# Norm sums of batches 2 and 3 moved beside the first `w_gate` jobs, and their result passed through a row in DRAM

## The chip, the cores and the metric

One Trainium2 chip, one of its cores. The metric is the device time of one execution in microseconds. The engines are called PE (TensorE, with its weight loads as PEld), DVE (VectorE), ACT (ScalarE), POOL (GpSimd) and SP (SyncE, which here only issues transfers).

## The reference

```python
# attention: batch 4, 12 heads, 448 tokens, head size 64
scores = scale * np.matmul(q, k.transpose(0, 1, 3, 2)) - np.log(S)
attn = 1.0 / (1.0 + np.exp(-scores))
x = np.matmul(attn, v)                # tokens x 768 after the heads are joined
# first gated layer, 768 -> 1536 -> 768
rms = np.sqrt(np.mean(x * x, axis=-1, keepdims=True) + 1e-06)
xn = x / rms * rms_g
g = xn @ w_gate
silu = g * (1.0 / (1.0 + np.exp(-g)))
x = silu * (xn @ w_val) @ w_out
# second layer, 768 -> 2048 -> 768
h = x @ w_in
out = (h - np.tanh(h)) @ w_out2
```

All of it in float32. The change concerns `rms`: one number for each of the 4 x 448 tokens.

## The kernel before

The tokens lie along the free dimension: a `unit` tile is 128 features by 448 tokens of one batch, so x of a batch is six units. The attention runs batch by batch, six pairs of heads each: line 612 makes scores, line 619 their sigmoid, line 642 the product with v. Each pair gives one unit of x. `x_end` squares it on ACT and adds it on DVE to a unit `sq`; for batches 2 and 3 it also spills x to DRAM (line 669).

Then the layers run in two halves, batches 0 and 1 and then 2 and 3 (`BATCHES`). A float32 product is three matmuls on a high and a low part of each operand. The work is a list of jobs: `seven_units` (line 978) makes two output chunks of `w_gate`, `w_val` or `w_in` for two batches with seven block products in place of eight, `set_units` (line 921) does the same for a set of `w_out` or `w_out2`, `plain_units` (line 1003) a set without that saving. The right factors of x for a half take 42 units (`xs`: 3 chunk pairs x 7 products x high and low part), those of a set 28 (`moe`: 2 x 7 x 2).

The norm of one batch is three functions. `norm(b)` multiplies the four 112-token pieces of `sq` with a column of ones (line 677, four float32 matmuls, which the trace shows as eight records), which leaves the sums as 112 x 4 numbers in a PSUM bank; DVE scales them (line 681), and POOL raises them to the power -0.5 into `rc` (line 683). `clear_norm(b)` writes the whole bank once (line 331). `spread_norm(b)` has to bring these numbers into a row along the free dimension on all 128 partitions: DVE makes diagonal pieces from the identity (line 698, four per batch), PE multiplies them with ones (line 702), and ACT copies the bank to a unit `rstd` (line 706). `x_whole` (line 770) then scales x by `rms_g` and `rstd` on DVE.

The order in which everything is issued is written out by a planner, the class `Plan`. Each operation is given to it with its engine, an assumed duration, what it reads and writes, and how long after its end its result is there (`after`; `LAND` and `FAR` for transfers). It keeps a clock per engine, starts what can start soonest, and among those within 150 ns the one with the earliest due time. Due times go back from PE's operations in program order, so PE keeps nearly that order. `plan.later` gives an operation a later due time. Operations up to `WINDOW` = 500 places behind the oldest open one may start, those that open a buffer of a kind in `CLOSELY` (`xr`, `sq`, `acc`, `accs`, `again`) only up to 120. Buffers come from shared pools: 72 units (`N_UNIT`) for all kinds of unit, each kind with a limit of its own (`sq` 3, `rstd` 2, `xs` 42), and eight PSUM banks. Every engine then runs its list in order and waits on semaphores.

What surrounds the change: `mixed` puts side work between the units of the attention, and the main loop puts the lists of `beside` between the units of the jobs from `j0` up to `j1`:

```python
    mixed(attn_units(3), [lambda: norm(2), lambda: clear_norm(2)], [u for j in range(AHEAD) for u in (*by_dve(conv(j)), lambda j=j: load(j + AHEAD))], rows_b[at[2]:])
    norm(3)
    clear_norm(3)
    gates.clear()
    ...
        (last["Av", BATCHES[0]], first["Ag", BATCHES[1]], [lambda: [spread_norm(b) for b in BATCHES[1]], *x_units("A", BATCHES[1], True)], BEHIND),
```

So the sums of batch 2 stand in the attention of batch 3, those of batch 3 right behind it, and both are spread much later, beside the last `w_val` job of the first half, ahead of the reloads of x (`reload_x`, line 713) and its scaling for the second half.

Of the kernel before, what the change touches and what calls it, by code (L numbers as in the profile page):

```python
# [8 lines left out]
F32 = mybir.dt.float32  # L9
# [12 lines left out]
P = 128  # L22
# [237 lines left out]
def tile_sigmoid_attention_moe_moe(  # L260
# [38 lines left out]
    def bank(kind="mm"):  # L299
        return slot(kind, ps_p, [P, 512], F32, "ps")  # L300
# [82 lines left out]
    def load(j):  # L383
        if j >= len(jobs) or jobs[j][1] != BATCHES[0] or jobs[j][3] or is_early(jobs[j][0], jobs[j][2]):
            return
        ph, _, i, _ = jobs[j]
        raws[j] = [load_raw(PAIRS[ph][0][2 * i + e]) for e in range(2)]
# [84 lines left out]
    def conv(j):  # L472
        if j >= len(jobs):
            return []
        ph, bs, i, blocks = jobs[j]
        if blocks in (SET, PLAIN):
            return set_factors(j)
        if (ph, i) in stored:
            return again_units(j)
        return pair_units(ph, i, raws.pop(j), j)  # L480
# [190 lines left out]
    def norm(b):  # L671
        sq = sqs.pop(b)
        ps = bank("nm")
        ms, rc = (Slot(None, lambda t=t: norm_p.tile([TK, 4], F32, tag=t, name=t)) for t in ("ms", "rc"))
        def sums(e):
            for i in range(4):
                nc.tensor.matmul(  # L677
                    ps.tile[:TK, i:i + 1], lhsT=sq.tile[:, i * TK:(i + 1) * TK], rhs=ones[:, 0:1], start=True, stop=True)

        add({"PE": (1500, False)}, sums, [sq["t"]], [ps["t"]], stream="norm")  # L680
        add(dve(4), lambda e: nc.vector.tensor_scalar(
            out=ms.tile, in0=ps.tile[:TK, :4], scalar1=1.0 / DM, scalar2=EPS, op0=ALU.mult, op1=ALU.add), [ps["t"]], [ms["t"]])
        add({"POOL": (950, True)}, lambda e: nc.gpsimd.tensor_tensor(out=rc.tile, in0=ms.tile, in1=expo, op=ALU.pow),
            [ms["t"]], [rc["t"]])
        rcs[b] = rc, ps

    def clear_norm(b):
        ps = rcs[b][1]
        add({"PE": (250, False)}, lambda e: whole_bank(ps.tile), [], [ps["t"]], stream="norm")

    def spread_norm(b):
        (rc, _), ps2 = rcs.pop(b), bank("nm")
        dg = unit("sq")
        r = rstd[b] = unit("rstd")

        def spread(e):
            for i in range(4):
                nc.vector.tensor_scalar(
                    out=dg.tile[:TK, i * TK:(i + 1) * TK], in0=id_sb, scalar1=rc.tile[:, i:i + 1], scalar2=None, op0=ALU.mult)

        def rows(e):
            nc.tensor.matmul(ps2.tile[:, :S], lhsT=ones[:TK, :], rhs=dg.tile[:TK, :], start=True, stop=True)  # L702

        add({"DVE": (760, True)}, spread, [rc["t"]], [dg["t"]])
        add({"PE": (1500, False)}, rows, [dg["t"]], [ps2["t"]], stream="norm")
        add(act(S, psum=True), lambda e: nc.scalar.copy(r.tile, ps2.tile[:, :S]), [ps2["t"]], [r["t"]])
# [344 lines left out]
    def attn_units(b):  # L1051
        units = []
        for at in range(b * HP, (b + 1) * HP, 2):
            for x in (at, at + 1):
                units.append(lambda x=x: pair_qk(*pairs[x], (0, 1)))
                units.append(lambda x=x: (get_ready(x + 3), pair_qk(*pairs[x], (2, 3))))
            for x in (at, at + 1):
                units.append(lambda x=x: (pair_av(*pairs[x]), pair_end(*pairs[x])))
        return units
# [29 lines left out]
    def by_dve(units):  # L1089
        def run(u):  # L1090
            plan.copies_by = "DVE"
            u()
            plan.copies_by = None

        return [lambda u=u: run(u) for u in units]

    def mixed(units, *others):


        at = [0] * len(others)  # L1100
        for u in units[:2]:
            u()
        units = units[2:]
        for n, u in enumerate(units):
            u()
            for k, o in enumerate(others):
                while at[k] < (n + 1) * len(o) // len(units):
                    plan.later = BESIDE
                    o[at[k]]()
                    plan.later = 0  # L1110
                    at[k] += 1
# [5 lines left out]
    mixed(attn_units(2), [lambda: norm(1), lambda: clear_norm(1), lambda: spread_norm(1), *x_units("A", BATCHES[0], False)], rows_b[at[1]:at[2]])  # L1117
    for j in range(AHEAD):
        load(j)
    mixed(attn_units(3), [lambda: norm(2), lambda: clear_norm(2)], [u for j in range(AHEAD) for u in (*by_dve(conv(j)), lambda j=j: load(j + AHEAD))], rows_b[at[2]:])  # L1120
    norm(3)
    clear_norm(3)
    gates.clear()


# [1 line left out]
    first = {(ph, bs): [j for j in range(len(jobs)) if jobs[j][0] == ph and jobs[j][1] == bs][0] for ph in ("Ag", "C") for bs in BATCHES}  # L1127
    last = {(ph, bs): [j for j in range(len(jobs)) if jobs[j][0] == ph and jobs[j][1] == bs][-1] for ph in ("Av", "C") for bs in BATCHES}
    beside = [
        (last["Av", BATCHES[0]], first["Ag", BATCHES[1]], [lambda: [spread_norm(b) for b in BATCHES[1]], *x_units("A", BATCHES[1], True)], BEHIND),  # L1130
        (last["Av", BATCHES[1]], first["C", BATCHES[0]], x_units("C", BATCHES[0], True), BEHIND),
        (last["C", BATCHES[0]], first["C", BATCHES[1]], x_units("C", BATCHES[1], True), BEHIND),
# [97 lines left out]
```

## Time and profile before

| | us |
|---|---|
| median of 3 runs | 1059.64 (1057.77 to 1060.39) |
| profiled execution | 1060.05 |
| its span, first to last instruction | 1058.2 |
| PE busy | 1045.9 |
| attention, up to about | 165 |
| first half of `w_gate`, `w_val` and `w_out` | about 165 to 400 |

The span is that of one profiled execution. Busy time counts a stretch once, also where matmuls overlap. In the chain of waits each piece starts where the one before it released it, so a piece of PE is the time that PE's stream really moved on. In the timeline a row is a run of like instructions, and the brackets hold how long the engine stood before it and what ended that. In the table of stretches the columns are the stretch and its length, the busy us of PE, PEld, DVE, ACT and POOL with their instructions, the granted clock (1.00 is full), the DMA engines' busy share and GB/s. `L324` and `L331` are helpers (copies, and the writing of a whole bank), `SPq` is SP's queue.

### The profile page before, as it was taken

How to read it: one execution, taken by the hardware profiler on the slowest of the kernel's cores; microseconds unless marked ns; L12 is line 12 of the kernel's file. 1: busy time of each engine (PE TensorE's matmuls, PEld its weight loads, DVE VectorE, ACT ScalarE, POOL GpSimd, SP SyncE). 2: the span in 40 equal slices, each digit the busy share in tenths (PEclk: the TensorE clock that was granted, in tenths of full speed). 3: DMA queues.
4: the chain of work that ended last, by engine and by line, in shares of the span. 5: the costliest groups of instructions: out<-in, count | busy, mean ns of one | idle time of the engine just before them, and what ended most of it. 6: DMA issues, size and time to landing. Idle time of an engine off the chain costs nothing.

```text
span 1058.2 us, 15120 instructions
## 1 busy us (share of the span) xinstructions
PE 1045.9 (99%) x5148; PEld 876.2 (83%) x5148; DVE 766.9 (72%) x1212; ACT 689.4 (65%) x1247; POOL 139.7 (13%) x194
## 2 busy tenths in 40 slices
PE   9999999999999999999999999999999999999998
PEld 3434447999999889999999989999988899999997
DVE  1328976975976895875885777888886888667756
ACT  5766765666675755665665656677675777666652
POOL 1211100000004022111113021000303120003030
PEclk9999999999999999999999999999999999999999
DMA  6888787766759979697879589557959891849393
GB/s 195 275 282 273 239 287 259 280 209 225 255 208 204 343 185 294 205 297 264 290 248 313 166 223 275 209 205 282 199 215 273 241 263 60 281 123 201 113 198 130
DMA packets 105869, 245.64 MB, mean 232 GB/s; under 512 B 27072, under 2 KB 59328, under 8 KB 105792
## 3 DMA queue, kind: packets, MB, share of 16 engines
q1 hardware_dynamic: 82224, 179.63, 50.2%
q0 software_dynamic: 23264, 64.89, 25.0%
q8 instruction: 40, 0.66, 0.3%
q14 instruction: 37, 0.30, 0.1%
q10 hardware_dynamic: 304, 0.16, 0.1%
HBM read 151.44 MB, written 93.19 MB: 231 GB/s over the span
## 4 chain that ended last, share of the span: by engine, by line
PE 88%; issue 5%; DMA 4%; DVE 1%; ACT 1%; POOL 1%; SPq 0%; POOLq 0%; DVEq 0%; ACTq 0%
PE ps L978 43%; PE ps L921 24%; PE ps L612 7%; PE ps L642 7%; PE ps L1003 5%; DMA out<-unit 2%; DMA cv<-wB 1%; DMA wt<-in_w_in 1%; PE ps L331 1%; DVE unit L857 1%; POOL out L795 0%; DVE unit L726 0%; PE ps L702 0%; PE ps L677 0%; ACT wt L324 0%
## 5 line engine op out<-in xcount | busy, mean ns | idle before, releaser
L978 PE MATMUL ps<-unit,wt 128*128 128x448 f32 x2520 | 522.1, 366 | 5.0 <-DVE unit L857 3.6
L978 PEld LDWEIGHTS ps<-unit,wt 128*128 128x128 f32 x2520 | 472.2, 188 | 48.5 <-DVE unit L857 4.7
L921 PE MATMUL ps<-unit,wt 128*128 128x448 f32 x1512 | 313.8, 366 | 0.0
L921 PEld LDWEIGHTS ps<-unit,wt 128*128 128x128 f32 x1512 | 283.8, 188 | 24.3 <-ACT ps L324 0.3
L407 DVE TENSOR_TENSOR wt<-cv,wt 128x768 fp32r<-128x768 f32 (+1 forms) x244 | 215.8, 892 | 76.1 <-ACT wt L324 70.9
L324 ACT CAST wt<-cv 128x768 fp32r<-128x768 f32 (+1 forms) x236 | 185.3, 787 | 108.3 <-PE ps L978 64.0
L324 ACT COPY unit<-ps 128x448 f32<-128x448 f32 x300 | 156.4, 534 | 130.0 <-PE ps L978 49.8
L726 DVE TENSOR_TENSOR unit<-unit 128x448 fp32r<-128x448 f32 x252 | 153.0, 620 | 28.9 <-ACT unit L324 13.4
L324 ACT CAST unit<-unit 128x448 fp32r<-128x448 f32 x252 | 137.9, 567 | 30.8 <-DVE unit L731 9.1
L857 DVE TENSOR_TENSOR unit<-ps,unit 128x448 f32<-128x448 f32 x168 | 103.5, 621 | 47.6 <-PE ps L978 27.6
L731 DVE TENSOR_TENSOR unit<-unit 128x448 f32<-128x448 f32 x144 | 87.4, 619 | 20.1 <-DMA unit<-sumB 10.2
L619 ACT ACTIVATE unit<-ps 128x448 f32<-128x448 f32 (+1 forms) x192 | 84.8, 582 | 6.2 <-PE ps L612 5.9
L612 PE MATMUL ps<-wt 64*128 64x448 f32 (+1 forms) x384 | 77.4, 546 | 0.0
L642 PE MATMUL ps<-unit,cv 128*64 128x448 f32 (+1 forms) x384 | 75.1, 542 | 0.0
L795 POOL DMA_DIRECT2D sumB<-unit x48 | 41.4, 945 | 255.0 <-DVE unit L857 157.2
L396 DVE SCALAR_TENSOR_TENSOR cv<-wt,zero 128x768 uint32<-128x768 uint32 x68 | 64.8, 953 | 11.6 <-ACT zero L324 6.6
L612 PEld LDWEIGHTS ps<-wt 64*128 64x128 f32 (+1 forms) x384 | 32.9, 173 | 39.6 <-issue 29.2
L642 PEld LDWEIGHTS ps<-unit,cv 128*64 128x64 f32 (+1 forms) x384 | 26.3, 136 | 47.5 <-issue 38.0
L1003 PE MATMUL ps<-unit,wt 128*128 128x448 f32 x288 | 60.3, 366 | 1.4 <-ACT unit L324 0.8
L324 ACT CAST zero<-wt 128x768 f16<-128x768 bf16 x52 | 56.1, 1078 | 8.6 <-DVE cv L396 4.6
L1003 PEld LDWEIGHTS ps<-unit,wt 128*128 128x128 f32 x288 | 53.8, 188 | 7.0 <-ACT unit L324 1.6
L665 DVE TENSOR_TENSOR unit<-unit 128x448 f32<-128x448 f32 x20 | 12.5, 623 | 62.3 <-ACT unit L658 62.3
(44 smaller groups left out, 427.1 us busy)
## 6 DMA issues: line engine op xcount, KB each, us to landing
wt<-in_w_out POOLq DMA_DIRECT2D x28, 768.0 KB, 7.4
cv<-wD SPq DMA_DIRECT2D x56, 384.0 KB, 4.9
cv<-wB SPq DMA_DIRECT2D x36, 384.0 KB, 5.4
wt<-in_w_in SPq DMA_DIRECT2D x16, 768.0 KB, 6.8
sumB<-unit POOLq DMA_DIRECT2D x48, 224.0 KB, 6.9
wD<-cv POOLq DMA_DIRECT2D x28, 384.0 KB, 5.6
wt<-in_w_gate SPq DMA_DIRECT2D x12, 768.0 KB, 5.1
wt<-in_w_val SPq DMA_DIRECT2D x12, 768.0 KB, 4.9
```

Source lines behind the costliest of these rows:

```text
L324: add(engines, lambda e: (nc.scalar.copy if e == "ACT" else nc.vector.tensor_copy)(to(), of()), reads, writes)
L396: add(dve(NW, psum=False), lambda e: nc.vector.scalar_tensor_tensor(out=c.tile.bitcast(U32), in0=r.tile[:, :NW, 1], scalar=13, in1=z.tile, ...
L407: add({**dve(n, psum=False), **pool(n)}, lambda e: ENG[e].tensor_sub(lo(), of(), hi().bitcast(F32)), [*reads, *kh], [*kl])
L612: nc.tensor.matmul(ps[i, c].tile[:n, :S], lhsT=t.tile[rows, at:at + n], rhs=t.tile[rows, :S], start=True, stop=True)
L619: add(act(S, psum=True), lambda e: nc.scalar.activation(to.tile[at:at + n, :S], ps.tile[:n, :S], AF.Sigmoid, bias=-math.log(S), scale=1.0 ...
L642: nc.tensor.matmul(ps.tile[i * D:(i + 1) * D, :S], lhsT=v.tile[:n, c, i, :], rhs=a[c][i].tile[:n, :], start=(c == 0), stop=(c == 3))
L726: add({**pool(S), **dve(S, psum=False)}, lambda e: ENG[e].tensor_sub(t["l"].tile, of.tile, t["h"].tile.bitcast(F32)), [of["t"], kh], [kl])
L731: add({**dve(S, psum=False), **pool(S)}, lambda e: ENG[e].tensor_sub(t.tile, x.tile, y.tile), [x["t"], y["t"]], [t["t"]])
L857: add(dve(S), lambda e: nc.vector.tensor_add(t.tile, ps.tile[:, :S], t.tile), [ps["t"], t["t"]], [t["t"]])
L921: nc.tensor.matmul(ps.tile[:, :S], lhsT=part(a), rhs=x[b].tile, start=n in (1, 5) and kp == 0 and q == 0, stop=kp == n_kp - 1 and q == 2, ...
L978: nc.tensor.matmul(ps.tile[:, :S], lhsT=part(a), rhs=x[b].tile, start=n in ((1, 2, 5) if opening else (1, 5)) and i == 0 and q == 0, stop= ...
L1003: nc.tensor.matmul(ps.tile[:, :S], lhsT=wt, rhs=a[p].tile, start=start and i == 0, stop=stop and i == 2, skip_group_check=True)
```

## The change

`norm` and `clear_norm` of batches 2 and 3 leave the attention and become four pieces of side work, spread evenly over the first two jobs (a `w_gate` and a `w_val` job). For these batches `norm` also writes `rc` to a row in DRAM with a transfer on SP, element by element, and `spread_norm` is one transfer on SP that loads this row to all 128 partitions of `rstd`. The diagonal pieces, the product with ones and the copy remain for batches 0 and 1 only. Places and due times of the later list in `beside` are as they were.

```diff
@@ norm(b), after the power
-        rcs[b] = rc, ps
+        if b in BATCHES[0]:
+            rcs[b] = rc, ps
+            return
+        d = Slot(None, lambda: dram_p.tile([1, S], F32, name=f"rstd{b}"))
+        rcs[b] = d, ps
+        add({"SP": (650, False)}, lambda e: nc.sync.dma_start(
+            out=d.tile.rearrange("o (i p) -> (o p) i", p=TK), in_=rc.tile), [rc["t"]], [d["t"]], after=15000)
@@ spread_norm(b), at its start
+        if b in BATCHES[1]:
+            d, _ = rcs.pop(b)
+            r = rstd[b] = unit("rstd")
+            add({"SP": (650, False)}, lambda e: nc.sync.dma_start(out=r.tile, in_=d.tile[0].partition_broadcast(P)), [d["t"]], [r["t"]], after=FAR)
+            return
@@ attention of batch 3
-    mixed(attn_units(3), [lambda: norm(2), lambda: clear_norm(2)], [u for j in range(AHEAD) for u in (*by_dve(conv(j)), lambda j=j: load(j + AHEAD))], rows_b[at[2]:])
-    norm(3)
-    clear_norm(3)
+    mixed(attn_units(3), [u for j in range(AHEAD) for u in (*by_dve(conv(j)), lambda j=j: load(j + AHEAD))], rows_b[at[2]:])
@@ beside
+        (first["Ag", BATCHES[0]], first["Ag", BATCHES[0]] + 2, [lambda b=b, f=f: f(b) for b in BATCHES[1] for f in (norm, clear_norm)], BEHIND),
```

## Rows read from the trace of the kernel before

**Rows 1.** The page, busy time of each engine, and TensorE's granted clock in 40 slices.

```profile
PE 1045.9 (99%) x5148; PEld 876.2 (83%) x5148; DVE 766.9 (72%) x1212; ACT 689.4 (65%) x1247; POOL 139.7 (13%) x194
...
PEclk9999999999999999999999999999999999999999
```

**Rows 2.** Who waited for whom, TensorE, whole span: us, times, longest us.

```profile
PE ps L978 <- DVE unit L857: 3.6, 3, 2.2
PE ps L331 <- POOL mark L1061: 1.9, 1, 1.9
```

**Rows 3.** The chain that ended last, attention of batch 3: start us, us, what.

```profile
124.71 5.46 PE ps L612 x28
130.17 0.88 PE ps L677 x8
131.05 0.93 PE ps L612 x4
...
138.14 3.96 PE ps L612 x20
142.10 0.29 PE ps L331
142.40 2.46 PE ps L612 x12
```

**Rows 4.** The same chain, where the attention ends and `w_gate` begins.

```profile
167.63 0.69 PE ps L677 x8
168.32 0.72 PE ps L978 x3
...
169.25 58.02 PE ps L978 x285
```

**Rows 5.** The same chain, end of the first `w_gate`/`w_val` half, batches 0 and 1.

```profile
319.88 8.05 PE ps L921 x40
...
329.47 14.55 DMA cv<-wB
...
359.14 0.76 PE ps L702 x2
359.90 0.61 PE ps L978 x3
...
361.26 3.87 PE ps L978 x19
```

**Rows 6.** Timeline, DVE, three places: start us, us, instruction [idle before, releaser].

```profile
168.36 0.16 DVE L681 TENSOR_SCALAR ms<-ps 112x4 f32<-112x4 f32 x1 [1.49 <-PE ps L677]
...
328.12 1.61 DVE L698 TENSOR_SCALAR unit<-id_sb,rc 112x112 f32<-112x112 f32 x8
...
361.59 1.27 DVE L770 SCALAR_TENSOR_TENSOR unit<-unit,g_sb 128x448 f32<-128x448 f32 x2
```

**Rows 7.** Groups by line, whole span: count, busy us, mean ns, idle before.

```profile
L683 POOL TENSOR_TENSOR rc<-ms,expo 112x4 f32<-112x4 f32 x4 | 4.7, 1167 | 36.9 <-DVE ms L681 36.9
...
L706 ACT COPY unit<-ps 128x448 f32<-128x448 f32 x4 | 2.1, 525 | 1.6 <-PE ps L702 1.6
```

**Rows 8.** Three stretches: engines' busy us (instructions), granted clock, DMA share, GB/s.

```profile
165.00:230.00 65.00, 65.00 (x324) 59.73 (x325) 51.79 (x83) 40.89 (x66) 1.01 (x1) 1.00 0.66 233
290.00:318.00 28.00, 28.00 (x140) 25.89 (x139) 21.17 (x33) 19.74 (x34) 0.00 (x0) 1.00 0.59 208
325.00:350.00 25.00, 22.84 (x113) 20.71 (x112) 15.02 (x30) 12.82 (x22) 7.22 (x10) 1.00 1.08 290
```

**Rows 9.** SP's transfers of lines 1073 and 713: duration, landing, min/median/max.

```profile
L1073 SPq DMA_DIRECT2D g_sb<-in_rms_g x1: 1831/1831/1831, 17.4 to 17.4; - x1
...
L713 SPq DMA_DIRECT2D unit<-x x12: 319/382/1247, 331.0 to 381.4; - x12
...
DMA to landing us min/median/max: 3.0/4.3/17.4
```

**Rows 10.** Timeline, SP, the first weight loads for set 0.

```profile
188.65 1.75 SPq L521 DMA_DIRECT2D cv<-wB  x2
```

## The prediction

> **What bounds the kernel now.** I read the page first, then the list of who waited for whom, then the chain of waits around the three places that the diff touches, then the rows of the moved and removed instructions. The page [rows 1] shows TensorE (PE) busy for 1045.9 of 1058.2 us, at the upper of its two clock levels (2.4 GHz) in every slice; VectorE (DVE) has 72%, ScalarE (ACT) 65%. Only 12.3 us are free of matmuls. Its longest named waits [rows 2] are 1.9 us at the start and one of 2.2 later. In the chain [rows 4] the `w_gate`/`w_val` products run 285 matmuls in 58.02 us, 203.6 ns each, without a wait. So TensorE in program order sets the time, and an instruction taken out of its stream is worth what it holds there, unless a wait behind it grows. One such wait stands near the change: the chain leaves TensorE there for a weight load, `cv<-wB`, issued at 329.47 us and 14.55 us on its way [rows 5], and behind it TensorE stands for the 2.2 us. The profiled execution took 1060.05 us, 1.85 more than its span; the three timed runs have their median 0.41 lower, at 1059.64. I sum against 1060.05 and take off 0.41 at the end.
>
> **What is removed: two diagonal products (batches 2 and 3).** In the chain [rows 5] the first starts at 359.14 and the matmuls behind the second at 361.26: 2.12 us, of which the three matmuls between them take 3 x 0.2036 = 0.61. So the two products hold TensorE for 1.51 us. They are the program's last use of line 702 in a stretch where the chain stays on TensorE, so I take all of it: -1.51. The ends are 0, if the time comes back as a wait, and -1.51. Off the path, DVE loses its 8 diagonal pieces, 1.61 us in all [rows 6], and ACT two copies of 525 ns [rows 7]. I count both at nothing: the chain at that time runs through the weight load, not through DVE.
>
> **What is moved: norm sums and clearing of batches 2 and 3.** Batch 3 is moved by little. In the trace it already stands between `w_gate` products [rows 4]: 167.63 to 169.25 is 1.62 us, less three matmuls (0.61) is 1.01 us for sums and clearing with what they cost at their edges. It keeps this price a few products later: 0. Batch 2 does leave the attention [rows 3]. There its sums take 0.88 us and split a run of score matmuls into 28 and 4, which take 5.46 + 0.93 = 6.39; by the runs of 28 and 12 (5.46 and 2.46, so 0.1875 each) an unsplit run of 32 takes 6.21, so the split costs 0.18. The clearing takes 0.29 and splits 20 from 12: 3.96 + 2.46 - 6.21 = 0.21 more. Together 1.56 us in the attention against 1.01 beside `w_gate`: -0.55. Ends: 0, if the new place costs the same, and -1.56, if it costs nothing. At the new place the sums wait for nothing, since both sums of squares are done before the first of these jobs.
>
> The in-order engines get new waits there. DVE's 160 ns scaling stood 1.49 us for the sums of batch 3 [rows 6]; batch 2 now adds one like it. Behind it stand conversions of weights and the closing of PSUM banks; DVE is busy 51.79 of 65 us in that stretch [rows 8], so 13 us of free time cover 1.5. Without that cover it would be 1.5 us of TensorE per batch. GpSimd's power (1.17 us [rows 7]) finds its engine idle: it is all that ran there in those 65 us [rows 8]. A norm bank stays taken from the sums to the clearing, some ten products or 6.5 us for each batch, beside the three banks of each of two overlapping jobs: seven of eight, so 0; if it comes up short, a product waits for one ACT copy, 0.53 us [rows 7].
>
> **What is added on SP's queue.** Per batch, one store of 448 numbers as single 4-byte pieces, and one load that spreads the row over 128 partitions. The trace has no such store. Its nearest rows [rows 9] are the reloads of x (0.32 to 1.25 us on SP, 3.0 to 17.4 us to landing) and the load of `g_sb`, 128 runs of 24 bytes: 1.83 us on SP. By the number of pieces the latter gives an estimate of 1.83 x 448/128 = 6.4 us, so a store holds SP for 0.3 to 6.4 us, plus a wait for GpSimd of a microsecond or two; I take 1.8, the `g_sb` row. Behind it are weight loads; the nearest to their use are the `cv<-wB` loads from 188.65 us [rows 10], wanted by the first set product, at 169.25 + 58.02 = 227.27 [rows 4]. That is 34 us of cover against at most 13 for both stores: 0. Without that cover SP's time would come straight onto TensorE.
>
> The spread load has the shape of the reloads of x, and I take their time. Its place matters more. The planner may start an operation up to 500 work items ahead of the oldest open one, but only 120 for the kinds it names (`xr`, `sq` and others), and `rstd` is not among them. The reloads, bound by 120, start at 331.0 [rows 9], 28 us before the diagonal products (359.14) that stand beside them in the program. By that ratio the spread loads start some 117 us ahead, near 242 us (an estimate; 331 is the late end). At the late end they would add 2 x 0.23 MB (128 x 448 x 4 bytes each) in the stretch where the DMA engines are full (1.08 of their time) and move 290 GB/s [rows 8]: 1.6 us, in front of the late `cv<-wB`. Early, they are out of that way: 0. Either way the row is in place before the first scaling of x, which DVE reaches at 361.59 [rows 6].
>
> **The sum**: -1.51 - 0.55 = -2.06, so 1057.99 for the profiled execution and 1057.6 for the median, 0.19% faster.
>
> **Page and trace.** [Rows 1] show 99% for matmuls but 83% for weight loads. The Trainium skill (Perfetto Trace Analysis, Identifying the Most-Contended Engine) says that matmul busy time is a bad measure of how close TensorE is to its limit, and that weight-load busy time is the better one. By that rule TensorE has room, taking matmuls out need not pay, and the sum would be 0; this is the second rival below.
>
> **The rivals.**
> A stall goes too. The load behind the wait of 2.2 us was issued at 329.47 [rows 5], and the order of SP's queue there is written anew, since eight DVE pieces leave and two loads appear earlier. If that load is issued some 3 us sooner, the wait goes: -2.06 - 2.2 = -4.3, so 1055.4. Against it: the planner counts a fixed time for each load and does not see the full DMA engines, and none of the removed work is in the chain before 344.
>
> No gain. If weight loads or other engines hand out the pace, the removed 2.06 us come back as longer waits: 1059.6. Weight loads cover 59.73 of 65 us in the `w_gate` stretch [rows 8], nearer to full than 83%, and the wait at 344 hangs on a load that the chain traces back to TensorE (8.05 us from 319.88 [rows 5]), so it would start earlier with it. Both speak against.
>
> Slower: the buffers run out. Loaded at about 242 us, the two rows hold two of 72 unit buffers until the scaling is done, over 100 us. Before, they were taken only by the copies behind the diagonal products. In between lies the preparation of a set: 42 buffers for the seven right factors of A (3 x 7 x 2) and 28 for those of a set (2 x 7 x 2) make 70, and the temporaries of the running products have the last two. If two fewer decide, one factor's high and low part wait until a phase of the set frees theirs: six products of three matmuls, 18 x 0.2036 = 3.7 us, at the set that begins about 307 us. That gives 1057.6 + 3.7 = 1061.3, and with two factors late 1065. Against it: TensorE is busy for all of 290 to 318 us [rows 8], and DVE and ACT have 7 and 8 of 28 us free. It decides from the point where a factor is still being split when its phase starts.
>
> **Chances.** My sum (with up to 1 us either way) 0.44, the stall gone too 0.22, no gain 0.16, slower 0.18. A change under 0.3% (3.2 us) cannot be told from none here. Faster by more: the stall gone, and an edge of my sum, 0.22 + 0.04 = 0.26. Slower by more: a little over half of the buffer rival, 0.11. The rest, 0.63, lies within. The range reaches from the stall gone with a microsecond more, 1054.4, to the buffer rival with one factor late and its spread, 1062.6.
>
> **What would show it.** Of line 702, four records fewer; L706 two; L698 eight. The score run of 32 is whole, and both sums stand between `w_gate` products at about 0.7 us each. TensorE's list of waits names nothing new between 165 and 345 us. The spread loads start before 300 us. The sum is wrong if TensorE's free time grows by more than a microsecond, above all before 346 us; the first rival is right if the wait on `cv<-wB` is gone, the buffer rival if TensorE waits for a split (lines 726, 731 or ACT's cast to a unit) at about 307 to 330 us.

## The result and the profile after

The change made the kernel slower. Its median is 1066.11 us (1064.20 to 1066.86, 6 runs), that of the kernel before on the same chip 1059.02 (1057.77 to 1060.39, 6 runs): a ratio of 1.0066, 95% interval 1.0054 to 1.0077. The forecast was 1057.6, at most 1062.6. The profiled execution took 1065.33 us with a span of 1063.5, where the one before had 1058.2.

The engines are as busy as in [rows 1], but the granted clock has one slice that is not full (page of the kernel after: busy time, and the clock in 40 slices).

```profile
PE 1046.2 (98%) x5144; PEld 876.8 (82%) x5144; DVE 764.2 (72%) x1204; ACT 687.9 (65%) x1245; POOL 139.6 (13%) x194
...
PEclk9999998999999999999999999999999999999999
```

TensorE's list of waits (us in total, times, longest) names what [rows 2] did not have: 5.4 us in one piece on ACT. `L989` is `L978` of before.

```profile
PE ps L989 <- ACT unit L324: 7.3, 3, 5.4
PE ps L989 <- DVE unit L868: 3.0, 4, 1.2
```

Where it stands is read from TensorE's timeline (start us, us, instruction, in brackets the idle time before it and what ended it). In [rows 4] the 285 products ran from 169.25 without a break.

```profile
167.19 0.36 PE L331 MATMUL ps<-mark 128*128 128x448 bf16 x1
173.00 15.73 PE L989 MATMUL ps<-unit,wt 128*128 128x448 f32 x63 [5.45 <-ACT unit L324]
188.58 0.85 PE L677 MATMUL ps<-ones,unit 128*112 128x1 f32 x8
...
211.74 3.53 PE L989 MATMUL ps<-unit,wt 128*128 128x448 f32 x16 [1.16 <-DVE unit L868]
```

The chain of the kernel after (start us, us, what) tells who held ACT: a `w_gate` load that took 10.77 us (the same load landed after 7.2 us before), then ACT's cast of it, then ACT's copy out of PSUM, for which the products wait. The last line belongs to the smaller wait at 211.74.

```profile
160.67 10.77 DMA wt<-in_w_gate
...
171.52 1.05 ACT zero L324
172.57 0.39 ACT unit L324
...
173.00 9.08 PE ps L989 x30
...
189.37 13.11 DMA wAv<-cv
```

The 30 matmuls took 9.08 us instead of 30 x 0.2036 = 6.11: 2.97 us more. The reason is in the stretches (the stretch, its length, busy us of PE, PEld, DVE, ACT, POOL, granted clock, DMA share, GB/s): behind the 5.45 us of standing the granted clock is 0.50, the lower of the two levels (1.2 GHz).

```profile
172.00:176.00 4.00, 3.00 (x8) 2.72 (x9) 0.00 (x0) 1.39 (x3) 0.00 (x0) 0.50 1.04 421
176.00:180.00 4.00, 4.00 (x14) 3.60 (x14) 3.16 (x5) 0.53 (x1) 0.00 (x0) 0.64 0.05 20
```

ACT works in order. First its timeline before, then after: the two `w_gate` casts, which stood 0.62 us and not at all for their loads, now stand 8.31 and 1.22, and the copies that empty PSUM stand behind them.

```profile
160.44 1.08 ACT L324 CAST zero<-wt 128x768 f16<-128x768 bf16 x1 [0.62 <-DMA wt<-in_w_gate]
...
166.12 1.06 ACT L324 CAST zero<-wt 128x768 f16<-128x768 bf16 x1
```

```profile
167.23 1.05 ACT L324 CAST zero<-wt 128x768 f16<-128x768 bf16 x1 [8.31 <-DMA wt<-in_w_gate]
...
171.52 1.05 ACT L324 CAST zero<-wt 128x768 f16<-128x768 bf16 x1 [1.22 <-DMA wt<-in_w_gate]
172.44 0.95 ACT L324 COPY unit<-ps 128x448 f32<-128x448 f32 x2
```

On SP's timeline the two loads left at 155.47 and 158.34 us before. After, the new store (line 690) stands ahead of them, and they leave at 157.80 and 160.67.

```profile
155.47 0.33 SPq L373 DMA_DIRECT2D wt<-in_w_gate  x1
158.34 0.33 SPq L373 DMA_DIRECT2D wt<-in_w_gate  x1
```

```profile
155.03 0.40 SPq L690 DMA_DIRECT2D rstd<-rc  x1
157.80 0.33 SPq L373 DMA_DIRECT2D wt<-in_w_gate  x1
160.67 0.33 SPq L373 DMA_DIRECT2D wt<-in_w_gate  x1
...
190.80 0.33 SPq L690 DMA_DIRECT2D rstd<-rc  x1
```

So SP holds the store for 0.4 us only. Its landing is what is long, and the DMA engines are busy with little to show for it (two answers for the kernel after: the store's line, and stretches as above):

```profile
L690 SPq DMA_DIRECT2D rstd<-rc x2: 332/366/401, 155.0 to 190.8; - x2
...
DMA to landing us min/median/max: 9.3/10.9/12.4
```

```profile
160.00:162.00 2.00, 2.00 (x12) 0.71 (x10) 1.84 (x4) 0.00 (x0) 0.00 (x0) 1.00 1.19 74
162.00:164.00 2.00, 2.00 (x12) 0.57 (x8) 1.44 (x2) 0.00 (x0) 0.00 (x0) 1.00 0.72 37
```

**The account.** I cut each profile at four marks of the chain: the first norm sums, the run of 108 set products near 231 us, the run of 100 `w_out` products near 381, the run of 117 near 1030. The first column needs a remark. The 16 opening matmuls take 352 to 581 ns each, and how many take the longer time differs from profile to profile, so the first sums start at 50.51 us in the first profile of before, at 49.64 in a second one and at 49.07 after. All kernels have this scatter; counted from the first sums, both profiles of before agree to 0.01 us at the next mark.

```
                          first sums  to set 0  to w_out  to the 117  to the end   span
before, first profile        50.51     180.44    150.60     649.04       27.6     1058.2
before, second profile       49.64     180.45    150.15     647.99       27.7     1055.9
after                        49.07     190.41    147.36     649.00       27.7     1063.5
move alone            (e1)   49.81     181.03    149.36     648.30       27.5     1056.0
before + one store    (e4)   50.06     186.91    149.96     648.60       27.2     1062.7
16-byte pieces        (e2)   49.64     182.21    147.61     650.45       27.7     1057.6
pieces 512 B apart    (e3)   49.18     181.29    147.21     648.32       27.7     1053.7
row, strided sums     (e8)   49.28     182.04    147.23     650.34       27.5     1056.4
move and row, strided (e8b)  50.36     183.20    147.30     649.17       27.8     1057.8
row, order on DVE     (e12)  49.56     180.44    148.44     648.51       27.9     1054.8
move and row, on DVE  (e13)  50.01     181.84    148.53     649.99       27.7     1058.1
sums spread by PE     (e10)  49.91     184.35    148.53     650.56       27.7     1061.0
```

After loses 9.97 us up to the first set: 5.45 of standing, 2.97 of lower clock, 1.16 of a later wait at 211.74 and 0.39 that is left over. The chain behind the later wait goes through a transfer `wAv<-cv` that left at 189.37, 1.4 us ahead of the second store, and took 13.11 us; e2 and e3, whose stores land sooner, have no wait there. It gains 3.24 in the next part; from there on the two differ by less than 0.1. That is +6.7 us; the medians differ by 7.1. (In e10 the first column is the first of its products; e5, e6 and the two probes are left out.)

### The profile page after: what moved, and what is told of

The parts are those of the page before. It is cut to its first block, busy times and chain, and to the rows that moved or that the text cites. A ratio compares the mean times of both kernels' runs of the same rounds, so it can differ in the third digit from the quotient of the medians.

```text
span 1063.5 us, 15092 instructions
## 1 busy us (share of the span) xinstructions
PE 1046.2 (98%) x5144; PEld 876.8 (82%) x5144; DVE 764.2 (72%) x1204; ACT 687.9 (65%) x1245; POOL 139.6 (13%) x194
## 4 chain that ended last, share of the span: by engine, by line
PE 74%; DMA 5%; DVE 3%; issue 1%; ACT 1%; POOL 0%; SPq 0%; DVEq 0%; ACTq 0%; POOLq 0%
PE ps L989 41%; PE ps L932 28%; PE ps L1014 5%; DMA wAv<-cv 3%; DMA wt<-in_w_gate 1%; DVE wt L407 1%; DMA wt<-in_w_in 1%; DMA out<-unit 1%; DVE unit L868 1%; DVE cv L396 0%; DMA cv<-wAg 0%; DVE unit L792 0%; POOL out L806 0%; ACT unit L324 0%; ACT wt L324 0%
## 5 line engine op out<-in xcount | busy, mean ns | idle before, releaser
L989 PE MATMUL ps<-unit,wt 128*128 128x448 f32 x2520 | 525.6, 367 | 10.3 <-ACT unit L324 7.3
L989 PEld LDWEIGHTS ps<-unit,wt 128*128 128x128 f32 x2520 | 474.1, 189 | 55.7 <-ACT unit L324 9.5
L742 DVE TENSOR_TENSOR unit<-unit 128x448 f32<-128x448 f32 x144 | 87.5, 619 | 19.4 <-DMA unit<-sumB 9.3
L488 DVE TENSOR_TENSOR cv<-cv 128x384 f32<-128x384 f32 x80 | 43.0, 553 | 17.6 <-DMA wAv<-cv 10.9
```

What stands on the lines that cost most here:

```text
L742: add({**dve(S, psum=False), **pool(S)}, lambda e: ENG[e].tensor_sub(t.tile, x.tile, y.tile), [x["t"], y["t"]], [t["t"]])
L989: nc.tensor.matmul(ps.tile[:, :S], lhsT=part(a), rhs=x[b].tile, start=n in ((1, 2, 5) if opening else (1, 5)) and i == 0 and q == 0, stop= ...
```

## The experiments

Theory S says that the store is to blame, theory R that the new order of the loads is. Ratios are to the kernel before on the same chip, with 95% intervals; the medians of before were 1057.9 to 1058.6.

**e1: the move alone.** Norms moved as in the change, but the spread is the old diagonal product, no row in DRAM.

```diff
@@ norm: kept for all batches
-        if b in BATCHES[0]:
-            rcs[b] = rc, ps
-            return
+        rcs[b] = rc, ps
+        return
@@ spread_norm
-        if b in BATCHES[1]:
+        if False:
```

> The changed kernel with the norm sums in their new place, but the numbers pass by the diagonal product as before, so no row in DRAM. Theory S (the store): a store of 448 four-byte pieces makes the loads behind it crawl for some 8 us, the w_gate load that ACT stands for comes 5 us late, and TensorE waits 5.5 us and then runs 3 us at the lower clock. Then this kernel shows none of it: 1056.5 to 1060 us, no wait of TensorE over 1.5 us near 168 us, clock 1.00 throughout. Theory R (the new order): the planner's new order puts the w_gate load 2.3 us later on SP and ACT's cast ahead of the copies that free PSUM, and this is the loss. Then the wait of about 5 us stays and the time is 1065 to 1068 us (the diagonal products, 1.5 us, are back too).

Measured: 1059.44, ratio 1.0010 [0.9998, 1.0023]. The 5.45 us are gone, so the move did not make them. But in the account it is 0.59 us later at the first set than before, where I had forecast 0.55 earlier. On its ACT timeline the `w_gate` cast already waits 3.00 us instead of 0.62:

```profile
162.65 1.07 ACT L324 CAST zero<-wt 128x768 f16<-128x768 bf16 x1 [3.00 <-DMA wt<-in_w_gate]
```

On SP its first load leaves at 157.53. Counted from the first sums that is 107.7 us, against 105.0 before and 108.7 in the change. So 2.8 of the 3.8 us by which the change issues this load later are the move's, and by them ACT stands 3.00 us at its cast before any store comes. TensorE's list names no wait there yet.

**e4: the kernel before and one store more.** One unused store of 448 four-byte pieces, right behind the spill of x that leaves SP at 153.7 us; the order on every engine stays otherwise as it was.

```diff
@@ x_end, behind the spill
+    one_store = lambda rc, x, d2=Slot(None, lambda: dram_p.tile([1, S], F32, name="more")): add({"SP": (650, False)}, lambda e: nc.sync.dma_start(out=d2.tile.rearrange("o (i p) -> (o p) i", p=TK), in_=rc.tile), [rc["t"], x[0], x[1]], [d2["t"]], after=15000)
...
+            (b, c) == (3, 3) and one_store(rcs[2][0], x)
```

> The kernel before with one store added and nothing else: batch 2's 112 x 4 numbers go to an unused row in DRAM, in 448 pieces of 4 bytes, issued on SP right behind the spill at 153.2 us, as in the changed kernel (155.0). All other orders are those of before. Theory S: the w_gate load issued 2 us later lands some 5 us late, TensorE waits 4 to 6 us near 168 us and loses some 3 us more at the lower clock: 1064 to 1069 us. Theory R: no difference from before, 1058.5 to 1060 us.

Measured: 1064.50, ratio 1.0051 [1.0032, 1.0070]. One store, in an otherwise unchanged order, brings most of the loss: 6.5 us up to the first set. The time is where theory S had it; the wait is 3.15 us, less than the 4 to 6 expected. TensorE's timeline in this kernel has it at the same place:

```profile
170.33 1.41 PE L677 MATMUL ps<-ones,unit 128*112 128x1 f32 x8 [3.15 <-DVE unit L665]
```

**e2 and e3: what of the store it is.** Both keep all orders of the change. e2 writes 112 pieces of 16 bytes into the same 1792 bytes; e3 writes 448 pieces of 4 bytes, but 512 bytes apart, and its load then reads a spilled x in place of the row, so the norm of batches 2 and 3 is left out there.

```diff
@@ e2, the store
-            out=d.tile.rearrange("o (i p) -> (o p) i", p=TK), in_=rc.tile), [rc["t"]], [d["t"]], after=15000)
+            out=d.tile.rearrange("o (p i) -> (o p) i", p=TK), in_=rc.tile), [rc["t"]], [d["t"]], after=15000)
@@ e3, the store
-        d = Slot(None, lambda: dram_p.tile([1, S], F32, name=f"rstd{b}"))
+        d = Slot(None, lambda: dram_p.tile([1, S * 128], F32, name=f"rstd{b}"))
...
-            out=d.tile.rearrange("o (i p) -> (o p) i", p=TK), in_=rc.tile), [rc["t"]], [d["t"]], after=15000)
+            out=d.tile.rearrange("o (i p w) -> (o p) i w", p=TK, w=128)[:, :, 0], in_=rc.tile), [rc["t"]], [d["t"]], after=15000)
```

> The changed kernel, every engine's order the same, but the store writes each partition's four numbers side by side: 112 pieces of 16 bytes in the same 1792 bytes. The row is then in another order than the tokens, so rms goes to the wrong tokens. Theory S with a price by the piece: a quarter of the crawl, 2 us, the w_gate load is nearly in time, TensorE waits at most 1.5 us at 168 us, 1056 to 1060 us. Theory S with a price by the place (many small writes into the same few hundred bytes): anything between, up to the whole 8 us. Theory R: no change, 1066 us, since no order differs.

> The changed kernel, every engine's order the same, but the store's 448 four-byte pieces lie 512 bytes apart in DRAM, and the load to rstd takes a spilled x of the same size, so rms is left out. Theory S with a price by the piece: no change, 1066 us, the loads behind the store still crawl for about 8 us. Theory S with a price by the place: pieces that share no bytes' neighbourhood do not wait for each other, the crawl goes, 1056 to 1060 us. Theory R: 1066 us.

Measured: e2 1059.04, ratio 1.0006 [0.9994, 1.0018]; e3 1059.02, 1.0008 [0.9992, 1.0024]. In both the wait shrinks, to 1.27 and 0.36 us, and the stores land in 2.3 to 5.7 us. e3 has as many pieces, and as small, as the change, so the number of pieces is not the cause. The same two stretches of e3 show the loads behind the store at 375 and 414 GB/s, against 74 and 37 in the change and 365 and 363 in the kernel before:

```profile
160.00:162.00 2.00, 2.00 (x14) 0.74 (x12) 1.84 (x4) 0.00 (x0) 0.00 (x0) 1.00 0.92 375
162.00:164.00 2.00, 2.00 (x12) 0.57 (x8) 1.64 (x4) 1.59 (x3) 0.00 (x0) 1.00 1.05 414
```

Neither is 2 us faster than before, so something else takes the time saved; the runs from e8 on ask for that.

**e7 and e11: the pieces by themselves.** Both put a probe behind the end of the kernel before: stores of 448 four-byte pieces at several spacings, each with a load of 384 KB behind it. In e7 the stores did not wait for one another.

```diff
@@ e11, behind the last store of the output
+        add({"SP": (650, False)}, lambda e: nc.sync.dma_start(out=dst(), in_=before.tile[:TK, 0:4]), [before["t"]], [d["t"]], after=15000)
...
+        add({"SP": (650, False)}, lambda e: nc.sync.dma_start(out=b.tile, in_=src.tile[:, 4 + n % 4]), [src[4 + n % 4], before["t"], d["t"]], [b["t"]], after=15000)
+        add({"SP": (650, False)}, lambda e: nc.sync.dma_start(out=b.tile[:TK, 0:4], in_=dst()), [d["t"], b["t"]], [b["t"]], after=15000)
```

> The kernel before, with a probe behind its last output: one after the other, stores of 112 x 4 four-byte pieces whose places in DRAM lie 512, 4, 8, 16, 32, 64, 128, 256, 512 and 4 bytes apart, each with a load of 384 KB issued right behind it, and each waiting for the landing of both before it. Theory S with a price by the place: the store at 4 bytes lands after 8 to 10 us and the load behind it as late; at 512 bytes 2 to 4 us, and the load as in the kernel (about 3 us when nothing else runs); somewhere between 16 and 128 bytes the price falls away. With a price by the piece all pitches take 8 to 10 us. Theory R: all pitches take 2 to 4 us. The kernel's time is longer by the probe, some 60 us.

> The kernel before with a probe behind its end, which adds time there: one after the other, each waiting for the one before, stores of 448 numbers of 4 bytes whose pieces lie 512, 4, 16, 32, 64, 128, 512 and 4 bytes apart, behind each a load of 384 KB and then a reload. Theory S (small pieces that fall into the same bytes of DRAM slow what comes behind them): the load behind the store of pitch 4 lands 5 us or more later than the one behind pitch 512, in both places, and between them it falls as the pitch grows. If it is the number of pieces alone: all eight alike within 1 us. If the slow part is only the store's own landing: loads alike, stores not.

e7 told nothing: its stores overlapped and landed in 11.5 us at 4 bytes but also in 11.5 at 16 and 14.1 at 32. e11 is chained. On SP's timeline each probe shows a store (L1179), the load 0.36 us behind it (L1182), and the reload, which waits for both (L1183):

```profile
1058.61 0.32 SPq L1179 DMA_DIRECT2D pitch_four<-cv  x1
...
1068.01 0.30 SPq L1183 DMA_DIRECT2D cv<-pitch_four  x1
1070.17 0.30 SPq L1179 DMA_DIRECT2D pitch_sixteen<-cv  x1
...
1074.94 0.30 SPq L1183 DMA_DIRECT2D cv<-pitch_sixteen  x1
...
1094.90 0.30 SPq L1179 DMA_DIRECT2D pitch_fivetwelve<-cv  x1
...
1098.86 0.30 SPq L1183 DMA_DIRECT2D cv<-pitch_fivetwelve  x1
1100.69 0.30 SPq L1179 DMA_DIRECT2D pitch_four_again<-cv  x1
...
1110.68 0.30 SPq L1183 DMA_DIRECT2D cv<-pitch_four_again  x1
```

From store to reload: 9.40 and 9.99 us at 4 bytes, 4.77 at 16, 4.33, 4.28 and 4.04 at 32, 64 and 128, and 3.96 at 512. The stores themselves landed after 7.4 and 7.3 us at 4 bytes, 2.7 at 16 and 1.9 at 512. The load behind the last 4-byte store landed after 9.6 us, behind the first store of 512 after 3.4 (the eight loads together):

```profile
L1182 SPq DMA_DIRECT2D cv<-wB x8: 423/490/492, 1053.1 to 1101.0; - x8
...
DMA to landing us min/median/max: 3.4/3.9/9.6
```

The number and the size of the pieces are the same in all of them. So it is the spacing, and a step between 4 and 16 bytes rather than a slope: 4.6 to 6 us for what stands behind such a store.

**e5 and e6: sums and spread in one product.** One product with ones in all 128x128 makes the sum on every partition, and GpSimd takes the power over 128x448; e5 for batches 2 and 3, e6 for all.

```diff
@@ norm(b), instead of column sums, clearing and diagonal product
+        add({"PE": (800, False)}, lambda e: nc.tensor.matmul(ps.tile[:, :S], lhsT=ones, rhs=sq.tile, start=True, stop=True), [sq["t"]], [ps["t"]], stream="norm")
...
+        add({"POOL": (3000, True)}, lambda e: nc.gpsimd.tensor_tensor(out=r.tile, in0=r.tile, in1=half, op=ALU.pow), [r["m"]], [r["m"], r["t"]])
```

> The kernel before, but for batches 2 and 3 one product of a 128 x 128 tile of ones with sq leaves the sums on all partitions; DVE scales that bank (0.62 us), GpSimd raises 128 x 448 numbers to -0.5, and one partition's row goes to DRAM as a single piece of 1792 bytes, to be loaded to all partitions later. No four-byte pieces, no diagonal product, no clearing. TensorE's stream loses 1.51 us of diagonal products and 2.57 us of sums and clearings and gains two products of 0.76 us with edges of some 0.1 to 0.2: -2.2 us. Theory S: no crawl behind a single piece, so 1055 to 1057 us beside 1058.2 before. Theory R (the planner's new order is what costs): the order is new here too, so a wait of some microseconds near 168 us and 1059 to 1063 us.

> As the kernel with the direct product for batches 2 and 3, but for all four batches (0 and 1 keep their row in a unit). Batches 0 and 1 give up 1.0 us of sums, 0.5 of clearing and 1.2 of diagonal product with the edges in the attention, each for one product of 0.76 with 0.2 of edge: -1.8 us each, so -5.8 us in all. Theory S: 1051 to 1055 us. Theory R: 1055 to 1061 us.

Both expectations missed: 1178.09, ratio 1.1131 [1.1117, 1.1146], and 1306.27, 1.2353 [1.2333, 1.2373]. The power's group in e5 says why (busy us, mean ns, idle before); on 112x4 it took 1.17 us [rows 7]. TensorE stands 53.95 us up to 223.75 and 59.91 us up to 308.29, each time while a power runs and 9 to 10 us beyond it. So e5 and e6 decide nothing between theories S and R.

```profile
L679 POOL TENSOR_TENSOR unit<-unit,half 128x448 f32<-128x448 f32 x2 | 144.5, 72232 | 24.7 <-DVE unit L677 14.1 <-ACT unit L621 10.6
```

**e8 and e8b: the row in pieces of 16 bytes and in token order.** Each column sum takes every fourth token. e8 leaves the norms where they were before; e8b moves them as in the change.

```diff
@@ norm, batches 2 and 3
-                    ps.tile[:TK, i:i + 1], lhsT=sq.tile[:, i * TK:(i + 1) * TK], rhs=ones[:, 0:1], start=True, stop=True)
+                    ps.tile[:TK, i:i + 1], lhsT=sq.tile[:, i * TK:(i + 1) * TK] if b in BATCHES[0] else sq.tile.rearrange("f (p i) -> f i p", i=4)[:, i], rhs=ones[:, 0:1], start=True, stop=True)
@@ norm, the store
+            out=d.tile.rearrange("o (p i) -> (o p) i", p=TK), in_=rc.tile), [rc["t"]], [d["t"]], after=15000)
```

> The changed kernel with the norm sums back where they stood before (batch 2 in the attention, batch 3 right behind it); the numbers still pass by a row in DRAM, and the sums take every fourth token, so that the row is written in token order as 112 pieces of 16 bytes. One part of the change alone, without the four-byte pieces. TensorE loses the diagonal products, -1.51. Theory S: 1056 to 1058 us beside 1058.2 before. Theory R: the order is new as soon as anything changes, 1059 to 1061 us, with runs that scatter by several microseconds as in the kernels with the moved sums.

> The change whole, with one thing mended: each column sum takes every fourth token, so that a store writes 112 pieces of 16 bytes in token order instead of 448 of 4. Theory S (the store's small pieces slow the weight loads behind it, the rest of the change is sound): 1057.87 - 2.0 = 1055.9 on the chip of the last call, ratio 0.998; no wait over 1.5 us at 168 us, granted clock 1.00 there. Theory R (the new order of SP's queue and of the planner costs what the diagonal products give): ratio 1.000 to 1.001, as in the three earlier kernels with the orders of the change. By the forecast's own sum without the store: 0.998.

Measured: e8 1058.62, ratio 1.0005 [0.9994, 1.0016]; e8b 1059.26, 1.0003 [0.9991, 1.0015]. No gain: by its ratio e8b stands where theory R had it. The account places it. From set 0 to `w_out` both save 2.8 to 3.4 us, as forecast and more; ahead of it e8 is 1.6 us late. That is the strided sums (TensorE's timeline of e8; 0.95 and 0.85 us in the kernel before):

```profile
128.87 1.81 PE L677 MATMUL ps<-ones,unit 128*112 128x1 f32 x8
...
167.11 1.61 PE L677 MATMUL ps<-ones,unit 128*112 128x1 f32 x8
```

0.86 + 0.76 = 1.62 us, against 1.60 in the account. Behind `w_out` up to 2.4 us more go. One place is at 576 us: e8's third `w_in` load leaves at 564.78 where the kernel before had it at 556.76, ACT's cast waits 4.35 us for it, and TensorE 0.89 (e8's timeline):

```profile
576.68 23.48 PE L989 MATMUL ps<-unit,wt 128*128 128x448 f32 x114 [0.89 <-ACT unit L324]
```

**e9: the kernel before once more.** Unchanged, for a second profile.

> The kernel before, unchanged, for a second profile of it. Open is where the 1.51 us of the two diagonal products went in the kernel with the row alone, whose profile showed 1056.4 us of span, 1.8 under the first profile of the kernel before (1058.2, with the 2.16 us wait behind the weight load at 344 us), while the medians of the two stood within 0.1%. If the 2.16 us wait at 344 us stood in that one execution only, this profile spans 1056 to 1057 us with a smaller wait there, and the 1.51 us are lost in waits elsewhere that come and go. If it is the kernel's own, it stands here too (1.5 to 2.5 us) and the span is 1058 again; then the saving is real in the trace and the medians hide it.

Span 1055.9, where the first had 1058.2. The wait at 344 us is there again, 1.69 us instead of 2.16: it belongs to the kernel. Neither case of the expectation holds whole, since the span is shorter all the same. 0.87 of the 2.3 us between the two profiles is the opening, 0.45 the wait at 344, the rest later waits (0.95 us at 768 in the first only).

**e10: one product, root on ScalarE.** For all batches: product with 1/768 in 128x128, root on ACT, reciprocal on DVE, the row as one piece of 1792 bytes.

```diff
@@ norm(b)
+        add({"PE": (800, False)}, lambda e: nc.tensor.matmul(ps.tile[:, :S], lhsT=parts_of, rhs=sq.tile, start=True, stop=True), [sq["t"]], [ps["t"]], stream="norm")
+        add({"ACT": (3200, False)}, lambda e: nc.scalar.activation(r.tile, ps.tile[:, :S], AF.Sqrt, bias=EPS), [ps["t"]], [r["m"]])
+        add(dve(S, psum=False), lambda e: nc.vector.reciprocal(r.tile, r.tile), [r["m"]], [r["m"], r["t"]])
```

> A version meant to beat both. Every norm in its old place, but the sum over the 128 partitions and its spread over them are one product with 1/768 in all 128x128, ScalarE takes the root with the epsilon and VectorE the reciprocal; batches 2 and 3 keep one row in DRAM as a single piece of 1792 bytes. TensorE loses per batch 0.88 us of sums, 0.29 of clearing and 0.75 of the diagonal product and gets one product of 0.75: 4 x 1.17 = 4.7 us, and some 0.4 for batch 2's split runs: 5.1 in all, so 1053 where the kernel before takes 1058, ratio 0.995, if ScalarE has room. Against it: each root needs another function table on ScalarE, 1.3 us to load and as much to go back, four times; between sigmoids whose products wait for PSUM these stand on the path, up to 4 x (2.6 + 0.6) = 13 us, ratio up to 1.008. Theory S expects no slow loads behind a store of one piece (landing about 2 us).

Measured: 1062.47, ratio 1.0037 [1.0024, 1.0049]: the counter-argument won, at about half of its upper price. TensorE has less work, but the first set starts 3.9 us late. Seven more loads of ACT's tables, 1283 ns each, and four reciprocals of 2.94 us stand between sigmoids and casts, and TensorE waits 1.29 us for a sigmoid at 140.89 and 1.38 for DVE at 180.81.

**e12 and e13: the row without strided sums.** The row stands in the order of its 16-byte pieces, and DVE reads it in token order as it scales x. e12 has the norms where they were before, e13 where the change has them.

```diff
@@ the store, in pieces of 16 bytes
+            out=d.tile.rearrange("o (p i) -> (o p) i", p=TK), in_=rc.tile), [rc["t"]], [d["t"]], after=15000)
@@ x_whole, batches 2 and 3
-            out=x.tile, in0=x.tile, scalar=g_sb[:, c:c + 1], in1=r.tile, op0=ALU.mult, op1=ALU.mult),
+            out=by(x.tile), in0=by(x.tile), scalar=g_sb[:, c:c + 1],
+            in1=r.tile if b in BATCHES[0] else r.tile.rearrange("f (p i) -> f i p", i=4), op0=ALU.mult, op1=ALU.mult),
```

> The row alone, norms where they were before, with the column sums taken as before; the row in DRAM is 112 pieces of 16 bytes and stands in the order of the pieces, and VectorE puts it in token order as it scales x. Counted from the first norm sums, so that the opening's scatter is out: the first set starts at 180.4 as in the kernel before (the kernel with strided sums: 182.0, because each of its two strided sums took 1.81 and 1.61 us instead of 0.95 and 0.85), then 2.8 us less to the 100 matmuls at 380 us (1.51 of the two diagonal products, the rest of the smaller wait at 344 us), and 1.0 more behind them (the wait at 576 us): -1.8 us in all, 1056.6 where the kernel before takes 1058.4, ratio 0.998. Theory 'strided sums took it': 0.998, norm sums 0.95 us each. Theory 'it comes back anyway': 1.000, as in the kernel with strided sums.

> The change whole, mended in the same way: pieces of 16 bytes, sums as in the change, token order made by VectorE. Against the kernel with the row alone it tells the price of the move by itself. By three profiles with these orders the first set starts 0.6 us later by the move and 0.3 to 1.3 later by the first w_gate load behind the store (counted from the first norm sums): -2.8 + 1.0 + 0.6 + 0.8 = -0.4 us, ratio 0.9996, and 0.0013 above the row alone. By the forecast's sum the move gives 0.55, so this one would be below the row alone by 0.0005.

e12: 1057.09, ratio 1.0000 [0.9991, 1.0009], its sums at 0.95 and 0.85 us and its first set at 180.44, as before. So the strided sums did take 1.6 us of e8, and the row by itself costs nothing there. From set 0 to `w_out` it saves 1.7 to 2.2 us. The times show no gain that can be told from none: the two products are worth 0.14%, and the interval, 0.09% to either side, has no room for all of it; the median lies 0.76 us (0.07%) under that of before. Two of its twelve runs lie 3 to 4 us above the rest, for which I have no cause. So the trace bears out 'strided sums took it', and the ratio 'it comes back anyway'. DVE pays for the order: the 24 scalings take 855 ns in the mean instead of 678, off the path.

e13: 1059.88, ratio 1.0021 [1.0012, 1.0030]. With the store and the sums mended, the kernel with the move is slower than the one without, by 2.8 us of the medians against e12. The strided pair does not show this: e8b and e8 stand at 1.0003 and 1.0005, though e8b's first set is 1.2 us later too. For e13 the account has 1.4 of it at the first set, of which 0.90 is the wait for the `w_gate` cast that the move made late (TensorE's timeline of e13), and 1.5 behind `w_out` (0.90 at 579 us, as in e8). In e12 the late `w_in` load came in time: ACT's cast waits 1.94 us for it, and TensorE not at all.

```profile
169.39 13.11 PE L991 MATMUL ps<-unit,wt 128*128 128x448 f32 x63 [0.90 <-ACT unit L324]
```

## Why the prediction was wrong

**The failed step is "What is added on SP's queue".** It priced each store by the time that it holds SP, took 1.8 us, and put against it "34 us of cover", up to the `cv<-wB` loads at 188.65 [rows 10], wanted at 227.27: "0". The hold was 0.4 us, inside the bounds. Three things were wrong. The store is not done when SP is: it lands in 9.3 to 12.4 us, and what is behind it on the DMA engines lands as late (the two `w_gate` loads after 9.3 and 10.8 us, where they took 4.9 and 7.2 before). The loads to look at were not the next ones that a set product wants, but the next ones that any in-order engine stands for: these two, issued 2.8 and 5.6 us behind the store. ACT already stood 0.62 us for the first of them in the kernel before; what spare time there was lay behind its cast. And the first store did not run beside the first jobs, where the program has it, but in the attention at 155 us, behind batch 2's sums at 141.05. e4 shows that the store alone suffices, e2, e3 and e11 that it is the 4-byte pieces lying side by side. The stall then cost half as much again by the lower clock, for which the sum had no term. With 16-byte pieces and otherwise the whole change (e2, e8b, e13) the ratio is 1.0006, 1.0003 and 1.0021 instead of 1.0066.

The Trainium skill (DMA: Bandwidth & Descriptors, Specifications) says that transfers under 512 bytes make a DMA engine read, modify and write. That rule goes by size and names no spacing; at one size e11 has 9.40 us side by side, 4.77 at 16 bytes and 3.96 at 512. No run here looks into the memory, so why side by side is slow stays open; that it is so, and that the loads behind suffer, is shown. The Trainium skill (DMA: Bandwidth & Descriptors, Rules for kernel authors) also advises to rearrange a strided last dimension so that it is contiguous. e2 and e12 did this for four numbers at a time: the stores then landed in 2.3 to 5.7 us and 3.0 to 3.5.

**The moved sums: -0.55, wrong in sign.** I counted two split runs in the attention and forgot that the order of everything around is written anew. In the change batch 2's sums still stand in the attention, at 141.05, its clearing stands at 167.19, and a run of score matmuls is now split by three `w_gate` products. Above all the first `w_gate` load leaves 2.8 us later. At the first set the move costs 0.59 us alone (e1), and 1.2 and 1.4 with the row (e8b against e8, e13 against e12); of the 1.4, 0.90 is the wait for that load's cast, and what makes the 0.59 is not shown. Over the whole kernel the three pairs disagree: the ratio changes by +0.0010, -0.0002 and +0.0021, and only the last is clear of noise. The sentence "the sums wait for nothing" was right and beside the point.

**The two diagonal products: -1.51, seen in the trace, not in the times.** The part from 231 to 381 us is 3.24 us shorter after. I made this 1.51, plus 1.46 by smaller waits (2.16, 0.18 and 0.59 before; 0.86, 0.23 and 0.38 after). The first rival, "A stall goes too", had the outcome by two thirds, but by luck: the wait at 344 went and a smaller one came at 366, yet the `cv<-wB` load left no sooner (98.9 us behind the set-0 mark, 98.5 before). It landed after 12.5 us instead of 14.5, and why stays open. The second rival, that nothing is gained where PEld has room, is not borne out at this place: in every kernel without these two products this part is 1.6 to 3.4 us shorter than in the two profiles of before, and 0.8 to 2.2 us shorter than in e1, which keeps them. Over the whole kernel the gain is not shown: behind `w_out` the kernels with the row take 648.3 to 650.6 us, those without 648.0 to 649.0, and e12, which has this saving and little else, stands at 1.0000.

**The spread load and the buffers: right.** The loads were issued at 266.7 us, where I had estimated 242. They land in 8 us, and TensorE waits for no split between 230 and 330 us. The rival that had the right sign, "the buffers run out", had the wrong mechanism.

**The bound: right,** and too short. TensorE in program order sets the time. But I read its waits and not how close to waiting its feeders were: [rows 2] show no wait at 165 us, while ACT already stood 0.62 us for a `w_gate` load there.

## What to carry to other kernels

Price a transfer by its landing and by what lands behind it, not by its issue; single 4-byte numbers side by side in DRAM are to be grouped into 16 bytes or more or set apart, and their order restored where an engine with spare time reads them. When a step is moved, look for the in-order engines that already stand for a load near its new place, since a planner shifts other loads with it. Before a profile of one execution is compared with another, take the opening out by a mark behind it.

## What was not expected of the hardware

- 448 pieces of 4 bytes, side by side in DRAM, delay the load behind them: in e11 it lands after 9.0 and 9.6 us, against 4.4 with the pieces 16 bytes apart and 3.4 and 3.5 at 512.
- After TensorE stood 5.45 us its granted clock was 0.50 (1.2 GHz) in the stretch from 172 to 176 us and 0.64 in the next, which cost 2.97 us. In e4, after 3.15 us, it was 0.58 from 170 to 174 us and 0.57 in the next stretch.
- GpSimd's power takes 72.2 us on 128x448, against 1.17 on 112x4.
- Weights read with a stride of 16 bytes nearly double the norm sums: 1.81 and 1.61 us against 0.95 and 0.85.
